# A three-bank rotation for the spatial sums, a split variance check and re-ordered last output blocks in the gMLP stage of a fused attention and gMLP kernel

## The chip, the core and the metric

The kernel runs on one core of a Trainium2 chip. The metric is the device time of one execution in microseconds (us). The kernel before was timed three times: 875.36, 876.12 and 876.20 us, so its median is 876.12 us. One further execution was profiled; it took 871.85 us by the same clock, and its profile spans 870.1 us from the first instruction to the last. All positions such as "at 763.97" below are microseconds from the start of that span.

## The reference, cut to what matters

The input is one sequence x of 2048 rows with 512 columns. A first stage, a recurrent attention over 64 segments of 32 rows, is added to x and gives h. The change doesn't touch it. The second stage is a gated MLP with a spatial mixing matrix:

```python
h  = x + attention(layernorm(x))
z  = gelu(layernorm(h) @ w_in)              # 2048 x 1792
z1 = z[..., :896]
z2 = layernorm(z[..., 896:])                # over the 896 columns
g  = einsum('ts,bsf->btf', w_sp, z2) + b_sp # spatial sums over all 2048 rows
out = h + (z1 * g) @ w_out                  # 2048 x 512
```

Each spatial sum needs z2 of every row, so none can be finished before the last row block of z2 has been normalised. Each output block needs all seven feature blocks of z1 * g for its rows.

## The kernel before, in words

Five engines run five instruction streams: TensorE (PE) multiplies, ScalarE (ACT) applies GELU and copies, VectorE (DVE) does the elementwise work, GpSimd (POOL) small powers, and SyncE (SP) issues all DMAs. The kernel is written as one long list of operations in program order. A small class, the Emitter, works out from the tokens that each operation reads and writes which operation of another engine has to be waited for. Each engine then executes its own operations strictly in that order. An operation that has to wait holds up everything behind it on its engine.

PSUM has eight banks of 512 fp32 columns, called bank 0 to bank 7. Each bank has one token, `PB(b)`. A matmul that starts a new sum in a bank waits until the engine that reads the bank's last sum has finished.

Constants: S = 2048 rows are RB = 16 row blocks of 128 and NTB = 4 time blocks of 512. The 896 features are FB = 7 feature blocks of 128.

**The loop over row blocks** (`for rb in range(RB)`, from L1111). For each row block it does the following:

- `z2_mm(rb, 0, ...)` and `z2_mm(rb, 1, ...)`: two groups of four matmuls (L1052) of 448 columns, each into the next bank of a rotation, each followed by a GELU on ACT (L1055). The rotation is `zbank()`: it counts up `zcnt` and returns 5, 6 or 7.
- `z2_norm(rb)`: statistics of z2 on DVE (L1065, L1067), then two POOL operations for the reciprocal root (L1069, L1071).
- `z2_apply(rb - 1)`: DVE normalises the previous row block (L1076).
- up to two `z1_group(tb, fb, zbank())`: four matmuls of 512 columns (L1083) and a GELU (L1086). There are 28 such groups in all. They are taken from a list from rb = 1 on. Those of the last time block wait for rb = 12.
- from rb = LAG = 4 on, five matmuls of spatial sums (`mix`, L1090): time block 0, feature blocks 0 to 4, row block rb - 4. These five sums stay open in banks 0 to 4 (ACC).

At rb = 0 and 1 the tail of the first stage is mixed in: the last attention row block is gathered (`F_group` L695 and `WoX_mm` L710), scattered (L720), added to h on DVE (`F_add`, L700), and its statistics follow (`h_done`, L724 to L728). Then, at rb = 1 and 2, `xn2_apply` (L733, DVE) normalises row blocks 14 and 15. At rb = 2 and 3, four PE transposes each (L1134) go into a `zbank()` bank, and `xn_copy` (L1048, DVE) copies that bank out.

The first-stage operation just ahead of the loop is a pair of sums (L660) in bank OB = 2 and bank OB2 = 6; ACT copies them out (`part_evac`, L672).

**After the loop**, for each of the five open sums in turn: four mix matmuls for row blocks 12 to 15, and then a `gate`. A gate is two DVE operations: L1096 reads the bank and adds b_sp, L1098 multiplies by z1.

**The loop over time blocks** (from L1169). For time block 0 the feature blocks 5 and 6 remain, in banks 7 and 5. For time blocks 1 to 3 feature block fb uses bank `fb % 2`, so feature block 6 of one time block and feature block 0 of the next both use bank 0. Each sum is 16 mix matmuls and a gate. After feature blocks 1 to 4 one pending output block of the previous time block is issued (`out_rb`, L1158 on): seven matmuls of 512 columns (L1161) into bank 2 or 3, a DVE addition of h (L1164) into one of two buffers `xn`, and a DMA to the output (L1166).

**The check.** After time block 0, `check()` multiplies all variances by zero on DVE (L1038; the result differs from zero if a variance isn't finite), reduces them (L1040), sums over partitions with one matmul of one column into bank 5 (L1041), and DVE writes a flag (L1043). All engines read the flag at their very end; if it were set, a general path would run.

**The end.** After time block 3, output blocks 12 to 15 are issued one after the other.

Of the kernel before, what the change touches and what calls it, by code (L numbers as in the profile page):

```python
# [10 lines left out]
ALU = mybir.AluOpType  # L11
# [158 lines left out]
def fast_path(nc, st, keep, A_x, A_mem0, A_Wq, A_Wk, A_Wv, A_Wo, A_seg_len, B_w_in, B_w_sp, B_b_sp, B_w_out, out):  # L170
    S = A_x.shape[1]
    D = A_x.shape[2]
# [6 lines left out]
    RB = S // 128  # L179
# [3 lines left out]
    FB = FH // 128  # L183
# [14 lines left out]
    def sb(name, shape, dt):  # L198
        return st.enter_context(nc.sbuf_tensor("f_" + name, shape, dt))
# [5 lines left out]
    def region(off, n):  # L205
        return arena[:, off:off + n]
# [27 lines left out]
    xn = sb("xn", [128, 2, 512], BF)  # L234
# [6 lines left out]
    onesrc = sb("onesrc", [128, 160], BF)  # L241
# [12 lines left out]
    okb = sb("okb", [128, 1], BF)  # L254
# [8 lines left out]
    ps = st.enter_context(nc.psum_tensor("f_ps", [128, 8, 512], F32))  # L263
# [5 lines left out]
    def PB(b):  # L269
        return ("ps", b)  # L270

    def sp(fn, **k):
        return em.add("sp", fn, dma=True, **k)

    def pe(fn, **k):
        return em.add("pe", fn, **k)
# [9 lines left out]
    def act(fn, **k):  # L286
        return em.add("act", fn, **k)

    def dve(fn, **k):
        return em.add("dve", fn, **k)  # L290
# [401 lines left out]
    def F_group(rb, bank):  # L692
        for j in range(4):
            i = (4 * rb + j) % 8
            pe(lambda e, i=i, j=j: e.matmul(ps[32 * j:32 * j + 32, bank, :], lhsT=F_sb[:, :], rhs=part[:, i, :], start=True, stop=False,  # L695
                                            tile_position=(0, 32 * j)),
               reads=[("part", i, 0), ("part", i, 1), "F"], writes=[PB(bank)])
# [16 lines left out]
    def WoX_evac(rb):  # L714
        act(lambda e: e.activation(out=partx[:], in_=ps[:, WXB, :], func=ACT.Copy), reads=[PB(WXB)], writes=["partx"])
# [127 lines left out]
    h_sb = region(RB * 512, RB * D).rearrange("p (rb d) -> p rb d", rb=RB)  # L843
    z1T = region(WSZ, FB * S).rearrange("p (fb t) -> p fb t", fb=FB)
# [3 lines left out]
    w_out = region(3 * WSZ + RB * 512, FB * D).rearrange("p (fb d) -> p fb d", fb=FB)  # L848

    def load_wT(tb, after):  # L850
        for t in range(8):
            sp(lambda e, t=t: e.dma_start(wTb[tb % 2][:, t, :, :], wT_d[8 * tb + t]), reads=[("wTd", 8 * tb + t)],
               writes=[("wT", tb % 2, t)], after=after)
# [4 lines left out]
    for s in range(NSEG):  # L858
        j4 = s % 4
        rb = s // 4  # L860
# [173 lines left out]
        return xts[rb // 8][:, rb % 8, :, :]  # L1034


    def check():
        dve(lambda e: e.tensor_scalar(out=okt[:], in0=mv[:, :, 1], scalar1=0.0, scalar2=0.0, op0=ALU.mult, op1=ALU.is_equal),  # L1038
            reads=[("mv", r) for r in range(RB)], writes=["okt"])
        dve(lambda e: e.tensor_reduce(out=okb[:], in_=okt[:], axis=AX.X, op=ALU.min), reads=["okt"], writes=["okb"])  # L1040
        pe(lambda e: e.matmul(ps[0:1, 5, 0:1], lhsT=okb[:, 0:1], rhs=onesrc[:, 0:1], start=True, stop=True),  # L1041
           reads=["okb", "onesrc"], writes=[PB(5)])
        dve(lambda e: e.tensor_scalar(out=flag[:], in0=ps[0:1, 5, 0:1], scalar1=128.0, scalar2=None, op0=ALU.not_equal),  # L1043
            reads=[PB(5)], writes=["flag"])
# [5 lines left out]
    def z2_mm(rb, hf, bank):  # L1050
        for dc in range(DC):
            pe(lambda e, dc=dc: e.matmul(ps[:, bank, 0:HF], lhsT=xT2(rb)[:, dc, :], rhs=w_in2[:, dc, hf * HF:(hf + 1) * HF],  # L1052
                                         start=(dc == 0), stop=(dc == DC - 1)),
               reads=[("w_in2", dc), ("xn2T", rb)], writes=[PB(bank)])
        act(lambda e: e.activation(out=z2[:, rb, hf * HF:(hf + 1) * HF], in_=ps[:, bank, 0:HF], func=ACT.Gelu_apprx_tanh),  # L1055
            reads=[PB(bank)], writes=[("z2", rb, hf)], after=[lastV])
# [23 lines left out]
    def z1_group(tb, fb, bank):  # L1080
        r0 = 4 * tb
        for dc in range(DC):
            pe(lambda e, dc=dc: e.matmul(ps[:, bank, 0:TB], lhsT=w_in1[:, dc, fb * 128:(fb + 1) * 128],  # L1083
                                         rhs=xts[r0 // 8][:, r0 % 8:r0 % 8 + 4, dc, :], start=(dc == 0), stop=(dc == DC - 1)),
               reads=["w_in1"] + [("xn2T", r) for r in range(r0, r0 + 4)], writes=[PB(bank)])
        act(lambda e: e.activation(out=z1T[:, fb, tb * TB:(tb + 1) * TB], in_=ps[:, bank, 0:TB], func=ACT.Gelu_apprx_tanh),  # L1086
            reads=[PB(bank)], writes=[("z1T", fb, tb)], after=[lastK])

    def mix(tb, fb, sc, bank):
        pe(lambda e: e.matmul(ps[:, bank, 0:TB], lhsT=z2[:, sc, fb * 128:(fb + 1) * 128], rhs=wTb[tb % 2][:, :, sc, :],  # L1090
                              start=(sc == 0), stop=(sc == RB - 1)),
           reads=[("z2", sc, 0), ("z2", sc, 1)] + [("wT", tb % 2, t) for t in range(8)], writes=[PB(bank)])
# [5 lines left out]
        dve(lambda e: e.tensor_tensor(out=z1T[:, fb, tsl], in0=gt[:, fb % 2, :], in1=z1T[:, fb, tsl], op=ALU.mult),  # L1098
            reads=[("gt", fb % 2), ("z1T", fb, tb)], writes=[("z1T", fb, tb)])

    zcnt = [0]

    def zbank():
        zcnt[0] += 1
        return 5 + zcnt[0] % 3

    act(lambda e: e.preload_act_table_set("gelu_apprx_tanh_and_others"))
    z1list = [(tb, fb) for tb in range(NTB) for fb in range(FB)]
    ACC = (0, 1, 2, 3, 4)
    LAG = 4  # L1110
    for rb in range(RB):  # L1111
        z2_mm(rb, 0, zbank())
        if rb == 0:
            F_group(RB - 1, XB)
        z2_mm(rb, 1, zbank())
        if rb == 0:
            for qr in range(4):
                WoX_mm(RB - 1, qr)
            endA = em.by_eng["pe"][-1]
            WoX_evac(RB - 1)  # L1120
            load_wT(1, [endA])
            sp(lambda e: e.dma_start(w_out, B_w_out.rearrange("(fb p) d -> p fb d", p=128)), writes=["w_out"], after=[endA])
        if rb == 1:
            WoX_scatter(RB - 1, XB)
            F_add(RB - 1, XB)
            h_done(RB - 1)
            for r in range(RB):
                sp(lambda e, r=r: e.dma_start(h_sb[:, r, :], h_d[r]), reads=[("hd", r)], writes=[("hs", r)], after=[lastQ])
        if rb in (1, 2):
            xn2_apply(RB - 3 + rb, rb % 2)  # L1130
        if rb in (2, 3):
            r, j, bank = RB - 4 + rb, (rb - 1) % 2, zbank()
            for dc in range(DC):
                pe(lambda e, dc=dc, j=j, bank=bank: e.transpose(out=psb[:, bank, dc * 128:(dc + 1) * 128], in_=xo[:, j, dc * 128:(dc + 1) * 128],  # L1134
                                                                identity=ident[:, :]), reads=[("xo", j), "ident"], writes=[PB(bank)])
            xn_copy(r, j, bank)
        z2_norm(rb)
        if rb > 0:
            z2_apply(rb - 1)
        for _ in range(2):  # L1140
            if rb >= 1 and z1list and (z1list[0][0] < 3 or rb >= 12):
                tb, fb = z1list.pop(0)
                z1_group(tb, fb, zbank())
        if rb >= LAG:
            for fb, bk in enumerate(ACC):
                mix(0, fb, rb - LAG, bk)
    z2_apply(RB - 1)
    while z1list:
        tb, fb = z1list.pop(0)
        z1_group(tb, fb, zbank())  # L1150
    for fb, bk in enumerate(ACC):
        for sc in range(RB - LAG, RB):
            mix(0, fb, sc, bk)
        gate(0, fb, bk)

    outr = out[0].rearrange("(rb p) d -> p rb d", p=128)

    def out_rb(rb):  # L1158
        bank = 2 + rb % 2
        for fb in range(FB):  # L1160
            pe(lambda e, fb=fb: e.matmul(ps[:, bank, 0:D], lhsT=z1T[:, fb, rb * 128:(rb + 1) * 128], rhs=w_out[:, fb, :],  # L1161
                                         start=(fb == 0), stop=(fb == FB - 1)),
               reads=["w_out", ("z1T", fb, rb // 4)], writes=[PB(bank)])
        dve(lambda e: e.tensor_tensor(out=xn[:, rb % 2, :], in0=ps[:, bank, 0:D], in1=h_sb[:, rb, :], op=ALU.add),  # L1164
            reads=[PB(bank), ("hs", rb)], writes=[("xn", rb % 2)])
        sp(lambda e: e.dma_start(outr[:, rb, :], xn[:, rb % 2, :]), reads=[("xn", rb % 2)])  # L1166

    pend = []
    for tb in range(NTB):  # L1169
        for fb in range(len(ACC) if tb == 0 else 0, FB):  # L1170
            bank = 5 + fb % 3 if tb == 0 else fb % 2
            for sc in range(RB):
                mix(tb, fb, sc, bank)
            gate(tb, fb, bank)
            if pend and fb >= 1:
                out_rb(pend.pop(0))
        if tb == 0:
            check()
        pend.extend(range(4 * tb, 4 * tb + 4))
        if tb + 2 < NTB:  # L1180
            load_wT(tb + 2, [])
    for rb in pend:
        out_rb(rb)

    for eng in Emitter.ENGS:
        em.add(eng, None, reads=["flag"])
# [761 lines left out]
```

The softmax here doesn't subtract the row's maximum and nothing guards it: scores larger than these inputs give would overflow.

## Time and profile before

| what | value |
|---|---|
| median of 3 runs, us | 876.12 |
| profiled span, us | 870.1 |
| busy share of the span: PE, PEld, DVE, ACT, POOL | 97%, 50%, 58%, 54%, 18% |
| mean granted TensorE clock | 0.998 |
| second stage: first L1052 to the end of the span, us | 687.15 to 870.1 |
| PE busy from 766.2 to 797.3, us of 31.10 | 30.36 |
| DVE busy in the same stretch, us of 31.10 | 11.76 |

"PEld" is the weight load of TensorE, which overlaps the matmuls. A row of the timeline gives start, duration, engine, line, operation and shapes, and at its end in brackets how long the engine sat idle before it and who ended that idle time. The chain that ended last is followed back from the last instruction; its pieces are given as start, duration and name. A matmul of 512 columns is shown as 379 ns long, but 32 of them in a row start within 6.90 us (766.19 to 773.09), that is every 0.2157 us: matmuls overlap. A gap between two matmuls is therefore best read from starts.

### The profile page before, as it was taken

The page shows a single profiled execution, that of the slowest core. Times are in us where ns is not written, and L with a number is a line of the kernel's source. Part 1 is how long each engine was busy: PE and PEld are TensorE (multiplying, and loading weights), DVE is VectorE, ACT ScalarE, POOL GpSimd, SP SyncE. Part 2 cuts the span into 40 slices and gives each one's busy share as a digit, 9 for nine tenths or more (in the row PEclk, how much of TensorE's full clock was granted, in tenths as well). Part 3 has the DMA queues.
Part 4 walks back from the last instruction along what each step waited for, and adds up shares of the span by engine and source line. Part 5 has one row for each costly group of instructions (what it writes and reads, how often), then busy time and mean ns, then how long its engine had stood idle before and what let it go on. Part 6 is the DMA issues. An engine that isn't in the chain of part 4 may idle for free.

```text
span 870.1 us, 45443 instructions
## 1 busy us (share of the span) xinstructions
PE 848.3 (97%) x22453; PEld 431.5 (50%) x18869; DVE 502.1 (58%) x1245; ACT 467.4 (54%) x1291; POOL 158.2 (18%) x427
## 2 busy tenths in 40 slices
PE   6999999999999999999999999999999999999997
PEld 6664545544455445554445445555454444444443
DVE  3446666666666666666666666666565554634443
ACT  3446666766666666656666666666666655200000
POOL 1712112121121212121122112121111122100000
PEclk9999999999999999999999999999999999999999
DMA  9972232213031222222241323333221870033001
GB/s 326 379 215 71 76 63 74 66 38 86 25 92 41 67 57 37 72 67 73 62 91 27 81 65 67 95 55 74 51 62 41 209 253 1 0 110 108 26 13 38
DMA packets 114038, 75.22 MB, mean 86 GB/s; under 512 B 70696, under 2 KB 99376, under 8 KB 113840
## 3 DMA queue, kind: packets, MB, share of 16 engines
q1 hardware_dynamic: 113840, 72.26, 30.1%
q8 instruction: 164, 2.69, 1.3%
q14 instruction: 34, 0.28, 0.1%
HBM read 39.46 MB, written 20.58 MB: 69 GB/s over the span
## 4 chain that ended last, share of the span: by engine, by line
PE 96%; DVE 2%; issue 1%; DMA 0%; ACT 0%; POOL 0%; SPq 0%
PE f_ps L280 30%; PE f_ps L660 13%; PE f_ps L281 13%; PE f_ps L1090 11%; PE f_ps L710 3%; PE f_ps L426 3%; PE f_ps L461 3%; PE f_ps L1052 3%; PE f_ps L1083 3%; PE f_ps L1161 3%; PE f_ps L574 3%; PE f_ps L625 3%; PE f_ps L631 1%; PE f_ps L554 1%; PE f_ps L681 1%
## 5 line engine op out<-in xcount | busy, mean ns | idle before, releaser
L280 PE MATMUL f_ps<-f_arena,f_hT 128*32 128x512 bf16 (+1 forms) x5120 | 352.8, 337 | 1.7 <-issue 0.6
L281 PE MATMUL f_ps<-f_arena,f_hT 128*32 128x256 bf16 (+1 forms) x3072 | 214.5, 308 | 0.0
L280 PEld LDWEIGHTS f_ps<-f_arena,f_hT 128*32 128x32 bf16 x5120 | 121.1, 96 | 169.0 <-issue 85.6
L518 ACT ACTIVATE f_Tst<-f_ps 128x512 bf16<-128x512 f32 (+1 forms) x320 | 149.9, 510 | 57.8 <-PE f_ps L280 54.1
L660 PE MATMUL f_ps<-f_arena,f_cT 128*32 128x256 bf16 x4096 | 133.5, 273 | 1.1 <-ACT f_cT L645 1.1
L597 POOL TENSOR_TENSOR f_E_sb<-f_R_sb,f_E_sb 128x64 bf16<-128x64 f32 x128 | 48.1, 376 | 378.2 <-ACT f_R_sb L589 378.2
L526 DVE STREAM_TRANSPOSE f_QT<-f_Tst 128x256 uint32<-128x256 uint32 x128 | 57.0, 446 | 94.9 <-ACT f_Tst L518 94.9
L660 PEld LDWEIGHTS f_ps<-f_arena,f_cT 128*32 128x32 bf16 x4096 | 92.0, 95 | 34.8 <-ACT f_cT L645 21.2
L1090 PE MATMUL f_ps<-f_arena 128*128 128x512 bf16 x448 | 101.3, 379 | 2.5 <-DVE f_arena L1096 1.6
L617 DVE TENSOR_SCALAR f_V_sb<-f_ps 128x512 bf16<-128x512 f32 (+1 forms) x128 | 70.6, 551 | 41.0 <-PE f_ps L280 41.0
L672 ACT ACTIVATE f_part<-f_ps 128x256 bf16<-128x256 f32 x128 | 49.2, 384 | 66.5 <-PE f_ps L660 66.5
L647 DVE TENSOR_SCALAR f_cT<-f_ps 128x160 bf16<-128x160 f32 (+1 forms) x192 | 61.0, 373 | 38.4 <-PE f_ps L631 38.4
L645 ACT ACTIVATE f_cT<-f_ps 128x160 bf16<-128x160 f32 (+1 forms) x192 | 53.0, 348 | 39.4 <-PE f_ps L631 39.4
L1090 PEld LDWEIGHTS f_ps<-f_arena 128*128 128x128 bf16 x448 | 43.6, 98 | 55.9 <-DVE f_arena L1096 2.6
L526 DVE STREAM_TRANSPOSE f_KT<-f_Tst 128x128 uint32<-128x128 uint32 (+1 forms) x192 | 66.0, 356 | 2.7
L585 ACT ACTIVATE f_R_sb<-f_ps 128x160 f32<-128x160 f32 x128 | 38.9, 304 | 33.6 <-PE f_ps L281 26.5
L1096 DVE TENSOR_TENSOR f_arena<-f_ps,f_arena 128x512 f32<-128x512 f32 x28 | 19.3, 690 | 57.8 <-PE f_ps L1090 57.8
L567 ACT ACTIVATE f_E_sb<-f_ps 128x224 bf16<-128x224 f32 x128 | 45.7, 357 | 0.0
L593 DVE TENSOR_TENSOR f_E_sb<-f_R_sb,f_E_sb 128x160 bf16<-128x160 f32 x128 | 44.7, 349 | 0.0
L589 ACT ACTIVATE f_R_sb<-f_R_sb 128x160 f32<-128x160 f32 x128 | 42.6, 333 | 2.0
L710 PE MATMUL f_ps<-f_arena,f_cTx 128*32 128x512 bf16 x512 | 40.5, 380 | 0.0
L280 PE MATMUL f_ps<-f_arena,f_hTe 128*32 128x512 bf16 x512 | 39.0, 382 | 0.0
(105 smaller groups left out, 1024.1 us busy)
## 6 DMA issues: line engine op xcount, KB each, us to landing
wT_d<-f_wst SPq DMA_DIRECT2D x32, 256.0 KB, 2.0
f_arena<-wT_d SPq DMA_DIRECT2D x32, 256.0 KB, 4.8
f_arena<-in_A_Wq_dram SPq DMA_DIRECT2D x4, 1024.0 KB
f_arena<-in_A_Wv_dram SPq DMA_DIRECT2D x4, 1024.0 KB
f_arena<-in_A_Wk_dram SPq DMA_DIRECT2D x4, 1024.0 KB, 15.9
f_arena<-in_A_Wo_dram SPq DMA_DIRECT2D x4, 1024.0 KB
f_Vx<-vext_d SPq DMA_DIRECT2D x128, 32.0 KB
f_xn<-in_A_x_dram SPq DMA_DIRECT2D x16, 128.0 KB, 2.2
```

The lines of the kernel that those rows point to most:

```text
L280: return e.matmul(out, lhsT=lhsT, rhs=rhs, start=start, stop=stop, skip_group_check=True, tile_position=pos)
L281: return e.add_instruction(mybir.InstMatmult(name=nc.get_next_instruction_name(), engine=mybir.EngineType.PE, ins=[e.lower_ap(rhs), e.lowe ...
L518: act(lambda e: e.activation(out=st_.rearrange("p (hp i r) -> p hp i r", i=32, r=2), in_=ps[:, bank, 0:64 * np_].rearrange("p (hp r i) -> ...
L526: dve(lambda e: e.transpose(out=dst, in_=src), reads=tok, writes=[(nm, b, k) for k in halves(b, p0, np_)])
L597: pool(lambda e: e.tensor_tensor(out=ev, in0=rv, in1=ev, op=ALU.mult), reads=[("R", b), ("Ex", b)], writes=[("Ex", b)])
L617: dve(lambda e: e.tensor_scalar(out=dst, in0=src, scalar1=VSC, scalar2=None, op0=ALU.mult), reads=[PB(bank)], writes=tok)
L645: act(lambda e: e.activation(out=dst, in_=src, func=ACT.Copy, scale=UNSC), reads=[PB(PVB[c])], writes=tok)
L647: dve(lambda e: e.tensor_scalar(out=dst, in0=src, scalar1=UNSC, scalar2=None, op0=ALU.mult), reads=[PB(PVB[c])], writes=tok)
L660: pe(lambda e, h=h, g=g, i=i, b=b, c=c: e.matmul(ps[32 * g:32 * g + 32, bank, 0:d1 - d0], lhsT=cTh[:, i, 8:40], rhs=w_o[:, h, d0:d1], star ...
L672: act(lambda e: e.activation(out=part[:, s % 8, d0:d1], in_=ps[:, bank, 0:d1 - d0], func=ACT.Copy), reads=[PB(bank)], writes=[("part", s % ...
L710: pe(lambda e, h=h, g=g, i=8 * qr + bg: e.matmul(ps[32 * g:32 * g + 32, WXB, :], lhsT=cTx[:, rb % 2, i, :], rhs=w_o[:, h, :], start=(i < 4 ...
L1090: pe(lambda e: e.matmul(ps[:, bank, 0:TB], lhsT=z2[:, sc, fb * 128:(fb + 1) * 128], rhs=wTb[tb % 2][:, :, sc, :], start=(sc == 0), stop=(s ...
```

## The change

Five edits, all in the second stage.

1. `check()` is split. `check_rows()` holds the two DVE operations and is issued at rb = 8. `check_all()` holds the matmul and the flag and is issued after time block 1 instead of time block 0. The matmul now has the ones as its stationary operand (128 columns) and writes 128 partitions.
2. `zcnt` starts at -1 instead of 0, so the rotation begins with bank 5 instead of bank 6.
3. z1 groups begin at rb = 2 instead of rb = 1.
4. After the loop, the mix matmuls of row blocks 12 to 14 are issued for all five sums; then come, for each sum, the matmul of row block 15 and the gate.
5. Time blocks 1 to 3 take banks 0, 1, 4 in rotation, running on across time blocks. At the end, output blocks 12 and 13 are opened with six of their seven matmuls each; then each gets its seventh and is finished. Block 14 goes to bank 6. Block 15 is done in two halves of 256 columns in banks 5 and 7, each with an addition and a DMA of its own.

```diff
-    def check():
+    def check_rows():
         dve(... okt ...)
         dve(... okb ...)
-        pe(lambda e: e.matmul(ps[0:1, 5, 0:1], lhsT=okb[:, 0:1], rhs=onesrc[:, 0:1], start=True, stop=True),
+
+    def check_all():
+        pe(lambda e: e.matmul(ps[:, 5, 0:1], lhsT=onesrc[:, 0:128], rhs=okb[:, 0:1], start=True, stop=True),
...
-    zcnt = [0]
+    zcnt = [-1]
...
-            if rb >= 1 and z1list and (z1list[0][0] < 3 or rb >= 12):
+            if rb >= 2 and z1list and (z1list[0][0] < 3 or rb >= 12):
...
+        if rb == 8:
+            check_rows()
...
+    for sc in range(RB - LAG, RB - 1):
+        for fb, bk in enumerate(ACC):
+            mix(0, fb, sc, bk)
     for fb, bk in enumerate(ACC):
-        for sc in range(RB - LAG, RB):
-            mix(0, fb, sc, bk)
+        mix(0, fb, RB - 1, bk)
         gate(0, fb, bk)
...
+    def out_done(rb, bank, d0=0, d1=D):
+        tok = [("xo_out", rb % 2, hf) for hf in range(2) if d0 <= 256 * hf < d1]
+        dve(lambda e: e.tensor_tensor(out=xn[:, rb % 2, d0:d1], in0=ps[:, bank, 0:d1 - d0], in1=h_sb[:, rb, d0:d1], op=ALU.add),
+            reads=[PB(bank), ("hs", rb)], writes=tok + [("xn", rb % 2)] * (rb < 2))
+        sp(lambda e: e.dma_start(outr[:, rb, d0:d1], xn[:, rb % 2, d0:d1]), reads=tok)
...
+    MB = (0, 1, 4)
...
-            bank = 5 + fb % 3 if tb == 0 else fb % 2
+            if tb == 0:
+                bank = 5 + fb % 3
+            else:
+                bank = MB[mcnt % 3]
+                mcnt += 1
...
-        if tb == 0:
-            check()
+        if tb == 1:
+            check_all()
...
-    for rb in pend:
-        out_rb(rb)
+    for rb in pend[:2]:
+        out_mm(rb, range(FB - 1), 2 + rb % 2)
+    for rb in pend[:2]:
+        out_mm(rb, (FB - 1,), 2 + rb % 2)
+        out_done(rb, 2 + rb % 2)
+    out_mm(RB - 2, range(FB), 6)
+    out_done(RB - 2, 6)
+    for d0 in (0, 256):
+        bank = 7 if d0 else 5
+        out_mm(RB - 1, range(FB), bank, d0, d0 + 256)
+        out_done(RB - 1, bank, d0, d0 + 256)
```

`out_mm(rb, fbs, bank, d0, d1)` issues the L1161 matmuls of feature blocks fbs and columns d0 to d1.

## The prediction

> **What bounds the kernel now.** I read the page first. Its row of busy times and its chain that ended last both name PE:
>
> ```profile
> PE 848.3 (97%) x22453; PEld 431.5 (50%) x18869; DVE 502.1 (58%) x1245; ACT 467.4 (54%) x1291; POOL 158.2 (18%) x427
> ...
> PE 96%; DVE 2%; issue 1%; DMA 0%; ACT 0%; POOL 0%; SPq 0%
> ```
>
> PE sets the end, and the change neither adds nor removes much PE work. It can only gain where PE stands still. So I next read the chain in order of time, from the last row block to the second time block (start, us, what):
>
> ```profile
> 752.61 0.52 DVE f_arena L1076
> 753.14 0.05 issue
> 753.18 10.76 PE f_ps L1090 x49
> 763.95 0.02 issue
> 763.97 0.70 DVE f_arena L1096
> 764.67 0.02 issue
> 764.70 0.69 DVE f_arena L1098
> 765.39 0.10 DVE f_okt L1038
> 765.48 0.02 issue
> 765.51 0.18 DVE f_okb L1040
> 765.69 0.04 issue
> 765.73 0.16 PE f_ps L1041
> 765.90 0.29 issue
> 766.19 7.07 PE f_ps L1090 x32
> ```
>
> PE stops for the z2 normalisation, runs 49 mix matmuls, and then waits for a whole gate, the two check operations and the check's own matmul. The timeline of PE gives the other stops of the second stage:
>
> ```profile
> 687.15 0.93 PE L1052 MATMUL f_ps<-f_arena 128*128 128x448 bf16 x4 [0.49 <-ACT f_part L672]
> ...
> 797.35 7.08 PE L1090 MATMUL f_ps<-f_arena 128*128 128x512 bf16 x32 [0.79 <-DVE f_arena L1096]
> ...
> 828.52 7.08 PE L1090 MATMUL f_ps<-f_arena 128*128 128x512 bf16 x32 [0.79 <-DVE f_arena L1096]
> ...
> 860.42 4.92 PE L1161 MATMUL f_ps<-f_arena 128*128 128x512 bf16 x22 [0.21 <-DVE f_arena L1098]
> ```
>
> The first is the loop's first matmul, in bank 6, which ACT is still emptying. The next two are time blocks that open bank 0 while its last gate reads it; the last is output block 12 waiting for the last gate. The stated idle times are too small by about 0.17, since they count from a modelled end that overlaps the next start. I use starts.
>
> [...]32 starts in 6.90 us, 0.2157 each. [...]opening bank 0 waits for L1096, and the trace shows just that releaser. [...]the output DMAs here show 1.7 us as their shortest landing.[...]
>
> **The change part by part**, in times of the profiled span. Plus is time saved.
>
> *Boundary of time blocks 0 and 1 (edits 1, 5).* 49 matmuls from 753.18 would end their starts at 753.18 + 49 x 0.2157 = 763.75; the next starts at 766.19. The new bank there is 0, whose gate was over at about 755, and the check is gone from there. **+2.44**.
>
> *Boundaries 1/2 and 2/3 (edit 5).* 789.49 + 32 x 0.2157 = 796.39 against 797.35: 0.96. 820.67 + 6.90 = 827.57 against 828.52: 0.95. With three banks no sum follows another in its bank before two sums of 3.45 us have passed, and a gate takes 1.4 us. **+1.91**.
>
> *The check (edit 1).* L1038 and L1040 (0.17 each) move to rb = 8 on DVE, ahead of statistics for which DVE sits idle 2.3 us per row block waiting for ACT: nothing. The flag operation (0.15) is behind the gate of feature block 6 on DVE; the next DVE work comes 3 us later: nothing. SP and POOL aren't passed. The matmul now stands between two mix matmuls with its inputs long ready. From below its price is a transposing matmul of 128 columns with its own weights, 0.22 / 4 = 0.055 (L1134, x4, 696.25 to 696.47); from above 0.3, its old row of 0.16 plus a start behind it. It can't be negative. I take **-0.10**, nearer the row with a full weight load in a stream.
>
> *Row block 15 (edits 3, 4).* Before, 8 mix matmuls from 750.69 end their starts at 752.41 and PE waits to 753.18: 0.77. After the last z2 matmul (its stream ends near 749.83) z2_apply needs until 753.12, 3.3 us. After the change PE has 8 z1, 5 mix and 15 mix matmuls to run there, 28 x 0.2157 = 6.0 us. **+0.77**. The five gates now come in a bunch: 5 x 1.33 = 6.65 us of DVE work. Behind them on DVE are the gates of feature blocks 5 and 6, ready 4.3 and 7.8 us after the first, and done by 9.4. They are in banks 7 and 5; the first mix that reuses a bank of the bunch, bank 0, comes at 7.8, after its gate; so nobody waits.
>
> *The start of the loop (edits 2, 3).* The first z2 matmul goes to bank 5, free long since. The L660 stream ahead, 26 matmuls from 685.73 at about 0.027, ends near 686.44, so the loop starts 687.15 - 686.44 = 0.71 earlier; F_group, which needs the L672 copy that ends at 687.09, is reached at 686.44 + 0.86. **+0.71**. But the two z1 groups at rb = 1 were cover. Count from the scatter L720 (692.67 before). DVE follows it: L700, statistics, then L733, which ends at 695.07, +2.40, so the transposes can't start before +2.45. PE now gets there at 0.33 + 1.51 = +1.84: it waits 0.61. Next, the transposes are the rotation's count 6, bank 5, and count 9, bank 5 again, is z2_mm(3, 0). PE reaches it at 2.45 + 0.22 + 1.73 = +4.40. The copy L1048 that empties bank 5 stands on DVE behind row block 1's statistics, L1076 and the second L733, back to back in the trace, and ends at 697.40, +4.73, visible at +4.77: 0.37. The moved groups run later at their old price. **-0.98**. Net -0.27; bounds +0.71 (both waits hidden) and -0.7 (only 0.49 gained at the start, both waits 0.1 longer).
>
> *The end (edit 5).* Count from the first closing L1161 (858.75). Before: last L1164 starts at 865.38, +6.63, ends +7.32. After: 12 matmuls take 2.59, and the gate ends at 860.37, +1.62: no wait, which alone would save 0.38. Then additions of 0.69: block 12 at 3.02 to 3.71, block 13 to 4.44. Block 14's sum is ready at 4.74, but it writes the buffer from which block 12's DMA, issued at 3.75, still reads. With the 1.7 landing it starts at 5.45 and ends at 6.15; on DVE both halves of block 15 queue behind it. They also need block 13's DMA, 4.50 + 1.7 = 6.2. A half addition is priced by the L617 rows, 0.69 for 512 columns and 0.41 for 256: 6.61, then 6.98. Saved: 7.32 - 6.98 = **+0.34**. PE isn't the bound: 14 matmuls of 256 columns are the same columns as 7 of 512 (no row shows this shape[...]). Bounds by landing: a first landing of 1.4 gives +0.6, 2.2 gives -0.2. SP issues one DMA more, about 0.46 apart (the L852 rows, 8 in 3.65), which delays the last by 0.1 at most. After the last addition the span runs 4.03 more; the last DMA is 64 KB, not 128 KB, and its data took about 0.5: **+0.15**, between 0 and 0.25.
>
> Sum: 2.44 + 1.91 - 0.10 + 0.77 - 0.27 + 0.34 + 0.15 = **5.24**. The span of 870.1 becomes 864.9. The unprofiled runs of before stand at 876.12, 6.0 above the span; I carry the difference over: 876.12 - 5.24 = **870.9**.
>
> **The rivals.** *The cover isn't missed* (0.13): DVE or the copies come early enough, and the start of the loop gains 0.71: 876.12 - 6.22 = 869.9. For it: small shifts on DVE; against: DVE is back to back there. *The last buffers wait longer* (0.07): landings nearer the 2.6 us median than 1.7 push the additions by some 0.9: 871.8. Against: before, block 14 had 2.2 us after block 12's issue and waited for PE alone. *The block boundaries hide a second wait* (0.05), so that edit 5 does not do what it says: the next time block's transposed w_sp isn't there and PE waits on; 4.35 of the gain is lost, 875.2. Against: SP issues those loads at 763.96 and 796.59, some 30 us ahead of use. *Slower, by the clock* (0.03): with the gaps gone PE runs some 165 us without a rest. Should its granted clock fall there, the price is 165 x (1/k - 1); it outweighs 5.24 below k = 0.969, and at 0.95 it is 8.7: 879.6. Against: the table of stretches grants 1.00 from 692.7 to 860.4, 57 us of them without a gap[...].
>
> **How the numbers follow.** Forecast 0.72, the rivals 0.13, 0.07, 0.05, 0.03. The bounds of start (+1.0, -0.4), end (+0.4, -0.7) and check (+0.05, -0.2) add to about 1.3 either way, and a median of a few runs moves by about 0.8. From 870.9 that gives 868.8 to 873.2, which holds the first two rivals too and leaves out the last two. Within 0.2% means within 1.75 us of 876.12, about what a measurement of this kernel can tell from no change: only the w_sp rival lies there. **Faster 0.92, same 0.05, slower 0.03.**
>
> **What would show it.** Right: no PE gap with releaser L1096 or L1040; no wait for L1076 after row block 15; the first L1052 about 0.7 earlier; PE waits of about 0.6 ahead of the first L1134 and 0.4 behind it; additions of blocks 14 and 15 that start after a DMA landing, not after PE. Wrong: any new gap of over 1 us between time blocks, a clock under 1.00, or a last addition later than 7.3 us after the last mix.

## The result, and the profile after

The changed kernel takes 870.97 us (median of 6 runs, 869.87 to 872.5). The kernel before, timed again with it, takes 875.74 (6 runs, 872.86 to 876.2). The ratio is 0.9956 with a 95% interval of 0.9937 to 0.9975, so 3.9 us are gained, between 2.2 and 5.5. (The means of the six fall by the same 3.9, from 874.99 to 871.13; the two medians lie 4.8 apart. Gains over before are taken from the ratios below, differences between two versions from their medians in one session.)

The page of the kernel after, busy times and chain:

```profile
PE 848.4 (98%) x22453; PEld 433.6 (50%) x18876; DVE 502.0 (58%) x1246; ACT 467.4 (54%) x1291; POOL 158.6 (18%) x427
...
PE 96%; DVE 2%; DMA 1%; issue 1%; ACT 0%; POOL 0%; SPq 0%; DVEq 0%
```

PE is busy as long as before (848.4 against 848.3). New is a DMA in the chain: 1% of the span.

The edits move the line numbers. In the kernel after, a z2 matmul is L1054 (L1052 before), a transpose L1136 (L1134), the copy behind it L1050 (L1048), `z2_apply` L1078 (L1076), a mix matmul L1092 (L1090), the first half of a gate L1098 (L1096), the check's matmul L1043 (L1041), an output matmul L1166 (L1161) and its addition L1172 (L1164). The kernels of the experiments are off by a few lines more.

The timeline of PE, kernel after (start, duration, operation; idle time ahead in brackets):

```profile
696.38 0.40 PE L1136 MATMUL f_ps<-f_ident,f_xo 128*128 128x128 bf16 x4 [0.44 <-DVE f_xo L733]
...
698.72 1.69 PE L1054 MATMUL f_ps<-f_arena 128*128 128x448 bf16 x8 [0.22 <-DVE f_arena L1050]
...
752.95 19.37 PE L1092 MATMUL f_ps<-f_arena 128*128 128x512 bf16 x89
...
795.47 0.17 PE L1043 MATMUL f_ps<-f_okb,f_onesrc 128*128 128x1 bf16 x1
795.49 2.75 PE L1092 MATMUL f_ps<-f_arena 128*128 128x512 bf16 x12
```

The 89 mix matmuls are one block: no wait for the last row block, none for the check, none for a bank. The check's matmul at 795.47 costs 0.03: the mix stream ahead of it would have gone on at 788.56 + 32 x 0.2157 = 795.46, and it goes on at 795.49. The first two rows are the two forecast waits at the loop's start.

The last pieces of the chain in order of time, kernel after (start, us, what):

```profile
856.14 2.77 PE f_ps L1166 x12
858.91 0.02 issue
858.93 0.70 DVE f_xn L1172
859.63 0.02 issue
859.65 0.58 DMA out_dram<-f_xn
860.23 0.02 issue
860.25 3.77 DMA out_dram<-f_xn
864.02 0.04 DVEq L158
864.05 0.04 issue
864.10 0.42 DVE f_xn L1172
```

Block 13's DMA is issued at 860.25 and lands (its completion is signalled) at 864.02, after 3.77 us; only then may block 15's addition write the buffer. Up to the last gates the waits went or came where they were forecast; the end didn't go as forecast.

Since the first stage varies by some us from one execution to the next (the last segment's L660 starts anywhere from 684.6 to 687.9, in kernels whose first stage is the same), I compare stretches. *Body* is from that L660 to the start of the first output matmul after the last mix matmul, called the first closing matmul; it is counted as the start of the last 32 mix matmuls plus 6.90, because single matmul records can be missing (of the 35 output matmuls behind the last mix matmul of the kernel after, 34 are recorded). *Last addition* (its end) and *span end* are counted from there. Each ratio is to before in the same session; before's median there is 875.74 (after), 875.15 (c0, e1, e2, e4), 876.33 (b0, e6, e8, e9), 874.17 (e5, e11, e13) and 874.58 (e15), so medians of different sessions aren't compared.

| kernel | body | last addition | span end | median us | ratio to before, 95% |
|---|---|---|---|---|---|
| before | 174.10 | 7.33 | 11.39 | 875.74 | |
| b0, before again | 174.11 | 7.34 | 11.72 | 875.46 | 0.9996, 0.9982 to 1.0009 |
| after | 169.46 | 8.94 | 13.64 | 870.97 | 0.9956, 0.9937 to 0.9975 |
| c0, after again | 169.46 | 9.16 | 13.45 | 871.01 | 0.9955, 0.9940 to 0.9970 |
| e1 | 169.46 | 7.34 | 11.36 | 869.70 | 0.9936, 0.9921 to 0.9952 |
| e2 | 169.46 | 6.69 | 10.85 | 869.01 | 0.9933, 0.9917 to 0.9949 |
| e4 | 168.46 | 6.69 | 11.21 | 868.00 | 0.9920, 0.9903 to 0.9936 |
| e5 | 173.87 | 7.33 | 11.89 | 871.88 | 0.9977, 0.9967 to 0.9988 |
| e6 | 175.76 | 8.95 | 13.30 | 877.47 | 1.0014, 1.0003 to 1.0025 |
| e8 | 171.69 | 7.33 | 11.53 | 872.79 | 0.9958, 0.9944 to 0.9971 |
| e9 | 170.08 | 8.90 | 13.20 | 872.82 | 0.9959, 0.9949 to 0.9969 |
| e11 | 175.42 | 7.33 | 11.64 | 872.93 | 0.9987, 0.9974 to 1.0000 |
| e13 | 174.07 | 7.33 | 11.81 | 873.70 | 0.9992, 0.9983 to 1.0001 |
| e15 | 169.46 | 6.84 | 11.85 | 869.45 | 0.9934, 0.9918 to 0.9951 |

The body shrank by 4.64 (forecast: 4.75). The end grew by 2.0, from the mean of before's two profiles (11.56) to that of after's two (13.54); the forecast was 0.49 shorter. That makes 2.6 us, but the times show 3.9. Two questions were open: what makes the end longer, and where the rest of the gain comes from.

### The profile page after: what moved, and what is told of

Same layout as the page of the kernel before. It is cut to its first block, busy times and chain, and to the rows that moved or that the text cites. A ratio compares the mean times of both kernels' runs of the same rounds, so it can differ in the third digit from the quotient of the medians.

```text
span 869.6 us, 45456 instructions
## 1 busy us (share of the span) xinstructions
PE 848.4 (98%) x22453; PEld 433.6 (50%) x18876; DVE 502.0 (58%) x1246; ACT 467.4 (54%) x1291; POOL 158.6 (18%) x427
## 4 chain that ended last, share of the span: by engine, by line
PE 96%; DVE 2%; DMA 1%; issue 1%; ACT 0%; POOL 0%; SPq 0%; DVEq 0%
PE f_ps L280 30%; PE f_ps L660 13%; PE f_ps L281 13%; PE f_ps L1092 11%; PE f_ps L426 3%; PE f_ps L710 3%; PE f_ps L461 3%; PE f_ps L1054 3%; PE f_ps L574 3%; PE f_ps L625 3%; PE f_ps L1085 3%; PE f_ps L1166 2%; PE f_ps L631 1%; PE f_ps L554 1%; PE f_ps L681 1%
## 5 line engine op out<-in xcount | busy, mean ns | idle before, releaser
L660 PE MATMUL f_ps<-f_arena,f_cT 128*32 128x256 bf16 x4096 | 133.9, 273 | 1.2 <-ACT f_cT L645 1.1
L660 PEld LDWEIGHTS f_ps<-f_arena,f_cT 128*32 128x32 bf16 x4096 | 92.4, 95 | 34.9 <-ACT f_cT L645 21.1
L1092 PE MATMUL f_ps<-f_arena 128*128 128x512 bf16 x448 | 100.6, 379 | 0.0
L1092 PEld LDWEIGHTS f_ps<-f_arena 128*128 128x128 bf16 x448 | 43.8, 98 | 52.7
L1098 DVE TENSOR_TENSOR f_arena<-f_ps,f_arena 128x512 f32<-128x512 f32 x28 | 19.3, 690 | 54.4 <-PE f_ps L1092 52.4
```

The source lines that it names most:

```text
L660: pe(lambda e, h=h, g=g, i=i, b=b, c=c: e.matmul(ps[32 * g:32 * g + 32, bank, 0:d1 - d0], lhsT=cTh[:, i, 8:40], rhs=w_o[:, h, d0:d1], star ...
```

## The experiments

Before each, the text says what was changed; "after" means against the changed kernel, "before" against the old one.

### c0: the changed kernel again

> The changed kernel once more, unedited. In its first profile the last addition ended 8.71 us after the first closing output matmul and the span 13.46 us after it (before: 7.32 and 11.35), because the DMA of output block 13 landed 3.77 us after its issue and the addition of block 15 waited for its buffer. Theory A (late landing by chance, a long wait only when one DMA engine is held by an instruction fetch): the last addition ends anywhere from 6.9 to 8.8. Rival B (a landing of over 3 us is what two output DMAs in a row always take): 8.5 or later again.

Last addition at 9.16, so the long wait is not a chance of one profile. (The 8.71 and 13.46 in the expectations were counted from the first recorded row, one matmul late; in the table they are 8.94 and 13.64.) Counted that way c0's is 8.94, above A's range and inside B's. One more profile can't tell whether the fetch or the close succession of the two DMAs is the cause; e15 below can.

### e1: the old ending in the changed kernel

```diff
-    for rb in pend[:2]:
-        out_mm(rb, range(FB - 1), 2 + rb % 2)
...
+    for rb in pend:
+        out_rb(rb)
```

> The changed kernel with the old ending: blocks 12 to 15 one after the other, block 15 whole. Theory A (the re-use of the two output buffers within about 1 us of the DMA's issue costs more than opening the sums early gains): last addition 7.3 us after the first closing matmul, span end 11.4 after it, and a time 0.5 to 2 us under the changed kernel's. Rival B (the end is no worse than forecast, 0.5 us gained): a time 0.5 us over the changed kernel's.

7.34 and 11.36, and 1.3 us under c0 in the same session (869.70 against 871.01). The waits of the additions at the end all have PE as releaser:

```profile
DVE f_xn L1172 <- PE f_ps L1166: 2.9, 4, 0.8
```

A was right: as built, the new ending loses.

### e2: four output buffers at the end

```diff
+        ob = xn
+        if rb >= RB - 2:
+            tok = [("xo_end", rb % 2, hf) for hf in range(2) if d0 <= 256 * hf < d1]
+            ob = xo
...
-        sp(lambda e: e.dma_start(outr[:, rb, d0:d1], xn[:, rb % 2, d0:d1]), reads=tok)
+        sp(lambda e: e.dma_start(outr[:, rb, d0:d1], ob[:, rb % 2, d0:d1]), reads=tok)
```

> The changed kernel with its new ending, but blocks 14 and 15 are put into a second pair of buffers (xo, free by then), so no addition at the end waits for a DMA. Theory A: the additions follow PE again, the last one ends about 6.6 us after the first closing matmul and the span 10.6 to 11.3 after it; time 1 to 2.5 us under the changed kernel's. Rival B (the last landing itself is late, whatever the buffers): last addition 6.6, but the span still ends 13 us after the first closing matmul and the time is the changed kernel's within 0.5.

The timeline of DVE at the end of e2:

```profile
860.40 1.29 DVE L1176 TENSOR_TENSOR f_xn<-f_ps,f_arena 128x512 bf16<-128x512 f32 x2 [1.39 <-PE f_ps L1166]
862.12 1.19 DVE L1176 TENSOR_TENSOR f_xo<-f_ps,f_arena 128x512 bf16<-128x512 f32 x2 [0.44 <-PE f_ps L1166]
863.65 0.42 DVE L1176 TENSOR_TENSOR f_xo<-f_ps,f_arena 128x256 bf16<-128x256 f32 x1 [0.34 <-PE f_ps L1166]
```

Every addition waits for PE alone; the last ends at 6.69. With the buffer wait gone, the ending is 0.5 us shorter than e1's in the profile; in the times (869.01 against 869.70, the intervals overlap) that isn't told apart. The half addition takes 0.42.

### e4: four buffers, and z1 groups from rb = 1

```diff
-            if rb >= 2 and z1list and (z1list[0][0] < 3 or rb >= 12):
+            if rb >= 1 and z1list and (z1list[0][0] < 3 or rb >= 12):
```

> As e2, and the z1 groups start at rb = 1 again, with the rotation still beginning in bank 5. Theory A (the groups at rb = 1 were cover for the transposes and for the copy out of bank 5): the PE waits of 0.61 and 0.37 us before and behind the first transposes vanish, the early start of 0.56 stays, so 1.0 us under e2. Rival C (the transposes or the copy stay late for another reason, or the groups at rb = 1 wait for a bank themselves): no gain over e2, within 0.3.

The timeline of PE at the loop's start in e4:

```profile
695.85 1.68 PE L1054 MATMUL f_ps<-f_arena 128*128 128x448 bf16 x8
697.36 0.39 PE L1136 MATMUL f_ps<-f_ident,f_xo 128*128 128x128 bf16 x4
697.58 1.89 PE L1085 MATMUL f_ps<-f_arena 128*128 128x512 bf16 x8
```

No wait is left. The body is 168.46 against 169.46, 1.0 us less, and the median is 1.0 us less: the intervals overlap, but the slowest of e4's executions (868.29) is under the fastest of e2's (868.59). The groups at rb = 1 were cover. This is the best version: 0.9920 of before, 0.9903 to 0.9936.

### b0, e6 and e8: before again, the new ending alone, the check split alone

> The kernel before once more, unedited, as a second profile. From the first L660 of the last segment (684.64 in the first profile) to the first closing output matmul it should again take 174.1 us, its last addition should end 7.3 us and the span 11.4 us after that matmul; the ratio should be 1.000. If instead the second stage or the end is longer by about 1.5 us than in the first profile, the first profile of before was a short one, and the times' larger gain (4.1 us for the changed kernel, where the traces show 2.3 to 2.6 from L660 to the end) is explained there; if not, it comes from the first stage.

Body and last addition are those of the first profile to 0.01 (the span's end comes 0.3 later), so the traces' second stages can be compared, and the larger gain in the times isn't explained by a short first profile.

e6 is before with `out_mm`, `out_done` and the new ending, banks and check untouched.

> The kernel before with the new ending alone. Theory A (the end loses by the wait for an output buffer): last addition 8.5 to 9.0 us after the first closing matmul, span end about 13.3 after it, and a time 0.5 to 2 us over before. Rival B (the ending gains 0.5 as forecast, and what e1 gained comes from elsewhere): 7.0 and 10.9, and a time 0.5 us under before.

Last addition at 8.95 and the time 0.14% over before (0.03 to 0.25%): theory A in the old surroundings too. But the body, in which nothing was changed, is 1.65 longer than before's. The table of stretches of e6 shows where (columns: stretch, sum, then busy time of PE, PEld, DVE, ACT and POOL, granted clock, DMA share, GB/s):

```profile
764.00:768.00 4.00, 2.20 (x11) 0.83 (x9) 1.79 (x5) 0.00 (x0) 0.00 (x0) 1.00 0.18 39
768.00:772.00 4.00, 3.74 (x11) 1.34 (x12) 0.15 (x1) 0.00 (x0) 0.00 (x0) 0.58 1.00 336
772.00:776.00 4.00, 4.00 (x20) 1.84 (x19) 1.38 (x2) 0.00 (x0) 0.00 (x0) 0.99 0.44 160
```

In the 4 us that follow the gap at the check PE is busy for 3.74 us and yet does 11 matmuls instead of 20: the granted clock is 0.58 there. The trace's clock record has it at one half from 768.64 to 772.06, 3.41 us; half of that, 1.7 us, is lost. The same gap stands in before and b0, whose clock stayed at 1.00 there. In before's profile the 4 us behind the gap read

```profile
768.00:772.00 4.00, 4.00 (x20) 1.77 (x19) 1.38 (x2) 0.00 (x0) 0.00 (x0) 1.00 0.84 292
```

So the 2.44 us gap may cost more than its length: in some executions 1.7 us more, if it is the gap that brings the fall. e8 and e13 test that.

e8 is before with the check split alone (`check_rows` at rb = 8, `check_all` after time block 1).

> The kernel before with the check split alone: the two DVE operations at rb = 8, the matmul after time block 1. Forecast's terms: the gap between time blocks 0 and 1, 2.44 us from start to start, is gone, since time block 1 opens bank 0, which nobody reads then; 2.4 us under before. Rival (the gate of feature block 6 still holds time block 1, by a token that I overlooked): a gap of about 0.95 stays, as at the other boundaries, and the gain is 1.5. The matmul of one column now stands behind the 32 mix matmuls of time block 1 and ahead of the wait for bank 0, so its own price is hidden here.

```profile
754.89 17.66 PE L1092 MATMUL f_ps<-f_arena 128*128 128x512 bf16 x81 [0.61 <-DVE f_arena L1078]
...
796.64 7.08 PE L1092 MATMUL f_ps<-f_arena 128*128 128x512 bf16 x32 [0.78 <-DVE f_arena L1098]
```

In e8's timeline of PE, the 49 matmuls and the 32 of the next time block have become one row of 81, with no gap; the other boundary's wait stays. The body is 2.42 shorter (forecast 2.44). The time is 3.7 us shorter, 2.5 to 4.9: more than the body, as for the whole change, though the interval only just leaves out the body's 2.42.

### e9: 40 small matmuls at PE's start

```diff
+    for _ in range(40):
+        pe(lambda e: e.matmul(ps[:, 5, 0:1], lhsT=onesrc[:, 0:128], rhs=onesrc[:, 0:1], start=True, stop=True),
+           reads=["onesrc"], writes=[PB(5)])
```

> The changed kernel with 40 small matmuls more at the very start of PE's program, where PE waits 6 us for its first input; nothing else differs. It asks what places the 16 KB instruction fetch that sits on one DMA engine while block 13's output leaves. Theory D (the fetches come at fixed steps of PE's program, every 255 or so of its instructions, so 80 instructions more move them by a third of a step): the fetch at the end comes some us earlier or later, block 13 lands about 1.7 us after its issue, the last addition ends about 7.0 after the first closing matmul, as forecast, and the time is 1 to 2 us under the changed kernel's. Rival E (the last fetches hang on PE coming to the end of its program): the fetch is again 5 to 6 us after the first closing matmul, block 13 lands at 3.8 to 4.1 and the last addition at 8.7 to 8.9.

The instruction queue q8 moved 164 packets of 16 KB in the kernel after, one for every 252 of the 41,329 instructions of PE and PEld; I take them for PE's fetches from that count. Theory D fell: the waits at the end of e9 are

```profile
DVE f_xn L1175 <- PE f_ps L1169: 2.6, 2, 1.4
DVE f_xn L1175 <- DMA out_dram<-f_xn: 2.0, 1, 2.0
```

and in the packet records the 16 KB fetch starts 5.36 us after the first closing matmul, against 5.33 in the kernel after. So it isn't placed by the number of instructions ahead of it; of the two theories that leaves E, PE's end. (The shift had a side effect: one row of L660 stands 0.6 us late there, in an otherwise equal body.)

### e15: PE's end put off by useless work

```diff
+    for _ in range(16):
+        pe(lambda e: e.matmul(ps[:, 0, 0:D], lhsT=onesrc[:, 0:128], rhs=w_out[:, 0, :], start=True, stop=True),
+           reads=["w_out", "onesrc"], writes=[PB(0)])
```

These stand behind the last output matmul of the changed kernel.

> The changed kernel with 16 useless matmuls of 512 columns (3.45 us, into the free bank 0) behind PE's last one, so that PE comes to the end of its program 3.45 us later while nothing that the output needs is moved. Theory E (PE's end calls the 16 KB fetch, which holds one DMA engine while block 13's output leaves): the fetch comes about 8.8 us after the first closing matmul instead of 5.3, block 13 lands 1.7 to 2 us after its issue, no addition waits for 2 us, and the last addition ends at 7.0 to 7.3 instead of 8.9. The span may still end late, since the fetch can now meet block 15's DMAs. Rival H (the second of two output DMAs 0.6 us apart lands late by itself): 8.9 again.

The timeline of e15's end:

```profile
859.63 1.29 DVE L1172 TENSOR_TENSOR f_xn<-f_ps,f_arena 128x512 bf16<-128x512 f32 x2 [1.39 <-PE f_ps L1166]
860.35 3.77 SPq L1174 DMA_DIRECT2D out_dram<-f_xn  x5
862.10 1.35 DVE L1172 TENSOR_TENSOR f_xn<-f_ps,f_arena 128x512 bf16<-128x512 f32 x3 [1.19 <-PE f_ps L1166]
862.57 3.23 PEld L1214 LDWEIGHTS f_ps<-f_arena,f_onesrc 128*128 128x128 bf16 x16
862.68 3.62 PE L1214 MATMUL f_ps<-f_arena,f_onesrc 128*128 128x512 bf16 x16
```

The three last additions run back to back, none waits for a DMA, and the last ends at 6.84, with the same two buffers as after. The DMA view of the 4 us from 858.9 shows blocks 12 and 13 going out, 0.6 us apart as in the kernel after, with no late tail and no fetch among them:

```profile
DMA  0000000000000000000000179950189950000000
q1 hardware_dynamic: 288, 0.26, 18.8%
```

H fell. A kernel that does 3.45 us more PE work takes 0.9934 of before (0.9918 to 0.9951) where the changed one takes 0.9955 (0.9940 to 0.9970). Theory E holds in what it was about: put off PE's end, and block 13 is no longer late. Its time for the fetch missed: the fetch comes 7.52 us after the first closing matmul, not 8.8. PE's last matmul starts 3.35 us later than in the kernel after (9.31 against 5.96), the fetch only 2.2 later, so that it comes 1.8 ahead of that matmul where it was 0.6 ahead. Why it doesn't keep its distance stays open.

### e13: the gap covered, not removed

```diff
+        for i in range(8):
+            pe(lambda e: e.matmul(ps[:, 6, 0:D], lhsT=onesrc[:, 0:128], rhs=w_out[:, 0, :], start=True, stop=True),
+               reads=["w_out", "onesrc"], writes=[PB(6)])
         pe(lambda e: e.matmul(ps[0:1, 5, 0:1], lhsT=okb[:, 0:1], rhs=onesrc[:, 0:1], start=True, stop=True),
```

> The kernel before with 8 useless matmuls of 512 columns (ones by w_out, into the free bank 6) ahead of the check's matmul, in the time in which PE waits there. They take 8 x 0.216 = 1.7 us, less than the 2.44 us gap, so the gap between the mix matmuls stays as long as it was; only PE's idle time in it shrinks below 0.8 us. Theory F (the long PE gap at the check makes the granted clock fall to half for 3.4 us in more than half of the executions, as in the profile of e6, which costs 1.7 us each time): no profile shows a clock of 0.5 between 765 and 780, the mean clock is 0.999 or more in nearly all executions, and the time is about 1 us under before's. Rival G (the clock fall has to do with e6's own code or with chance elsewhere): the time is before's within 0.3 and the same share of executions shows 0.998 or less.

The table of stretches of e13, where the mix matmuls pause from 764.4 to 766.82:

```profile
764.00:768.00 4.00, 3.62 (x17) 1.57 (x17) 1.78 (x5) 0.00 (x0) 0.00 (x0) 1.00 0.59 163
768.00:772.00 4.00, 4.00 (x21) 1.77 (x19) 1.39 (x2) 0.00 (x0) 0.00 (x0) 1.00 0.94 327
```

The body is as long as before's (174.07), and the clock stays. A fall lowers the mean clock of the span by 3.41 x 0.5 / 872 = 0.002. The mean is 0.998 or less in none of e13's 22 executions and in 28 of the 51 of before in the same session; those 28 average 875.1 us, the other 23 average 873.1. In the session of e8 it is 31 of 53 for before (877.1 against 875.1 us) and 1 of 10 for e8, which has the same ending and no gap. So the clock part of theory F is shown: the open gap brings the falls. Its time is not: e13's ratio puts it 0.7 us under before instead of 1, with an interval from 0.1 over to 1.5 under. Its executions average 873.7, above the 873.1 of before's executions without a fall; why, stays open. Nor does the small session of c0 show the price: 8 of its 12 executions of before are at 0.998 or less, and they average 875.3 against 875.2.

The mean clock is a rough sign. It also counts the end of the span, where the clock is at one half some us after PE's last matmul (in before's profile from 867.52, 2.6 us after that matmul's start; in the kernel after from 865.87, 4.0 us after it, to the span's end at 869.6, which alone makes 0.002). So it can be compared only between kernels with the same ending. Before's own first profile reads 0.998 without a fall at the gap, and with the new ending 16 of e9's 20 executions do, though its profile shows no fall but that at the end.

### e5 and e11: the rotation alone, the loop's start alone

e5 is before with `bank = (0, 1, 4)[((tb - 1) * FB + fb) % 3]` for time blocks 1 to 3.

> The kernel before with the banks 0, 1, 4 in rotation for time blocks 1 to 3 alone; the check stays behind time block 0 with its gap. Forecast's terms: 0.96 + 0.95 at the boundaries 1/2 and 2/3, so from the first L660 to the first closing matmul 172.2 us instead of 174.1, and 1.9 us under before. Theory F adds: the clock falls stay as frequent as in before. Rival: a wait for w_sp's next block shows once the bank no longer waits, and less is gained.

Its profile has a clock fall (3.41 us from 768.99): 173.87 - 1.70 = 172.17, a gain of 1.94 (forecast 1.91). The time is 2.0 us shorter, 1.0 to 2.9. No wait for w_sp shows. Its mean clock was 0.998 or less in 7 of 22 executions, less often than before's 28 of 51, where as often was expected; the gap is the same, and whether that is chance isn't told.

e11 is before with `zcnt = [-1]` and `rb >= 2`.

> The kernel before with edits 2 and 3 alone: rotation from bank 5, z1 groups from rb = 2. From the changed kernel's traces: 0.56 gained at the first L1052, 1.0 lost by the waits at the first transposes and behind them; and at row block 15, where one more z1 group (0.86) now runs under the z2 chain, the wait of 0.77 nearly vanishes, since 16 matmuls of 3.45 us cover 3.36. Sum 0.3 us under before, which the times will hardly show; from the first L660 to the first closing matmul 173.8 instead of 174.1. Rival (the z1 groups at rb = 1 weren't cover): 1.3 us under.

With a clock fall again (from 767.96), 175.42 - 1.70 = 173.72: 0.4 gained, as expected; the times (0.9974 to 1.0000) don't contradict it.

## Why the prediction was right, and where it wasn't

The predicted time, 870.9, and the measured one, 870.97, lie closer together than the working deserves, and that is luck. A gain of 5.24 was forecast, from a before at 876.12; by the ratio it is 3.9, from a before whose median was now 875.74. Two errors of opposite sign cancel in part (the end came 2.5 us worse than forecast, some 0.9 us by the clock was left out), and the spread of a few executions did the rest. One of the prediction's own signs of being wrong came, a last addition later than 7.3. Term by term:

- *Boundary 0/1, +2.44:* e8 measures 2.42. Right in place and size, but not the whole worth of that gap, as below.
- *Boundaries 1/2 and 2/3, +1.91:* e5 measures 1.94. Right. No second wait, for w_sp, came up.
- *The check's matmul, -0.10:* -0.03.
- *Row block 15, +0.77:* no wait for L1078 is left, as forecast. e4 shows that the new order of the mix matmuls is enough for it: with z1 groups from rb = 1 again the wait doesn't return.
- *The start of the loop, -0.27:* -0.44. Both waits came where they were put: L720 to the transposes 2.46 (forecast 2.45), to z2_mm(3, 0) 4.80 (forecast 4.77). Mis-sized was the early start: from L660 to the first z2 matmul 2.51 before, 1.95 after, so 0.56 and not 0.71, since PE now goes on 1.95 us after the stream's start where I had reckoned 1.80.
- *The end, +0.34 and +0.15:* -2.0 in all. **This is the step that failed: the landing of block 13's DMA.** Block 14's addition started 5.48 us after the first closing matmul (861.40; forecast 5.45), released as PE and block 12's landing came together. The next term was "4.50 + 1.7 = 6.2" for block 13's landing; it came at 8.10, 3.77 us after an issue at 4.33. I had bounded the landing at 2.2 from before, where each addition came late enough not to see it. The rival *the last buffers wait longer* names the mechanism, but with 2.6 us and 0.9 too small a size.
- *What the 1.7 missed:* of block 13's 144 packets 135 are through within 1.3 us of its issue. The other nine, one sixteenth, come only when an instruction fetch of 16 KB is over that takes 1.6 us (861.25 to 862.83): 15 of the DMA's 16 completions are signalled by 861.92, the last at 864.02. By my estimate from 144 / 16 = 9 the nine are the share of one of the core's 16 DMA engines; the trace doesn't name a packet's engine. In the kernel after, the DMA view from 860.2 to 864.2 has the fetch as the single packet of the instruction queue, and a thin tail of few packets near its end (busy tenths and GB/s in 40 slices of 0.1 us):

```profile
DMA  0017996017995000000000000002999410000000
GB/s 0 0 51 266 369 420 195 10 51 256 532 369 174 10 0 0 0 0 0 0 0 0 0 0 0 0 10 92 328 369 348 134 31 21 20 31 10 0 0 0
...
q8 instruction: 1, 0.02, 2.5%
```

The first two bursts are blocks 12 and 13, 0.6 us apart; the burst after the empty stretch is block 14, and the thin tail behind it ends near 863.9, just ahead of the landing at 864.02. e9 shows that the fetch doesn't move with the start of PE's program (5.36 us after the first closing matmul against 5.33), and e15 that it moves with PE's end, if not step for step (2.2 us later for an end 3.35 later). What at PE's end calls for it isn't shown. Nor does the packet record show all of the delay: in c0 the fetch is recorded from 6.20 to 7.13, half a microsecond after the other packets of block 13 were through at 5.66, and the last nine still come later, with the landing at 8.33; what held them until 6.20 isn't shown. With the new ending the DMA that meets the fetch is block 13's, whose buffer block 15 needs; before, the fetch came at 6.02, while block 14's DMA (issued at 5.85) was under way, and nobody waited for that buffer.

- *The rival by the clock* had the sign turned round. I feared that PE without rests would be slowed; here it is a rest that can slow it. The profiles with the gap show a fall to one half in 3 of 5 (e5, e6, e11), those without an open gap in none of 8 (e15's trace has no clock record). Taking 1.7 us in some 28 of 51 executions, I estimate that the split check is worth about 0.9 us more than its gap. Body 4.64, end -2.0 and clock 0.9 add to 3.5, inside the measured 2.2 to 5.5. I had compared with one profile in which the clock hadn't fallen, and so could not see it.
- *The spacing of 0.2157* held: the 32 matmuls in 6.90 us and the row of 89 run at 0.2157 each.

## What to carry to other kernels

When sums are opened ahead of a wait, follow what leaves behind them: here PE's last matmul started 0.3 us earlier (5.96 after the first closing one instead of 6.22), and a pair of output buffers, ample while blocks came 1.5 us apart, became the bound; two more buffers, or the old spacing, were worth 1.3 to 2.0 us. When a wait at the end of a loop is covered in two ways, take the one that needs no filler from elsewhere: moving the z1 groups cost 1 us at the start for cover that the new order of the mix matmuls gave by itself. And price a PE gap like this one of 2.44 us at its length plus what the clock may do behind it (here 1.7 us, by my estimate in some 28 of 51 executions): one profile without a fall doesn't show that there is none, and the mean clock of many executions helps only between kernels with the same ending.

## What was not expected of the hardware

A PE gap of 2.44 us, with one tiny matmul in it, can lower the granted clock to one half for 3.41 us, by the mean clock in about half of the executions of before (28 of 51, 31 of 53); covering it with 1.7 us of useless matmuls kept the mean clock at 0.999 or more in 22 of 22. And the end of one engine's program reached into the kernel's own DMAs: a 128 KB output that was under way during a 16 KB instruction fetch of 1.6 us landed 3.77 us after its issue, where 1.7 us is the shortest landing here; with PE's end put off by 3.45 us of useless work (e15) no addition waited for a landing.
